# A first batch whose position bias and mask enter the scores as matrix products

## The chip, the cores and the metric

The kernel runs on one core of one Trainium2 chip. The metric is the device time of one execution in microseconds (us), less is better. Five engines work side by side, each through its own queue in order: TensorE (PE: matrix products and, as PEld, the loading of their stationary operand), VectorE (DVE), ScalarE (ACT), GpSimd (POOL) and SyncE (SP). POOL and SP also issue the DMA transfers here: POOL those that convert float32 to bfloat16 on the way, SP the plain ones.

## What is computed

Attention with a sliding window and a linear position bias, and behind it an MLP mixer that works first over tokens, then over channels:

```python
# q, k, v: (8 batches, 8 heads, 576 tokens, 64); window = 128, scale = 1/8
rel    = pos[:, None] - pos[None, :]
bias   = slopes[:, None, None] * (-abs(rel))             # slope of head h: 2 ** -(h + 1)
mask   = (rel >= 0) & (rel < window)
scores = where(mask, scale * q @ k.T + bias, -1e9)
attn   = softmax(scores)                                 # written out with exp, sum, divide
x      = (attn @ v), heads side by side                  # (8, 576, 512)
h      = relu(x.T @ w_tok1) @ w_tok2                     # over tokens, 576 -> 256 -> 576
u      = x + h.T
out    = u + relu(u @ w_ch1) @ w_ch2                     # over channels, 512 -> 1536 -> 512
```

## The kernel before

The 576 tokens of a batch are four blocks of 128 (kb, qb = 0..3) and a tail of 64. A block of queries sees two blocks of keys. A score tile is named Skbj: key block kb for the four heads of half j, 1024 columns in two PSUM banks (the last key block, kb = 3, also holds the tail's scores). ScalarE takes the exponential of a whole tile (into `pe`), and VectorE multiplies it by `masks` (into `pb`), which holds exp(-slope * distance) inside the window and 0 outside. `masks` is made once, by eight exponentials on ScalarE (names M0 to M3, two each) from `dist`, which GpSimd makes (J). `maskt` holds its columns for the tail (m0, m1, on VectorE).

Nothing is scheduled by a planner: the order is written by hand, as strings of names, one string for the start (PROLOGUE), one each for batch 0 with the rest of the start (FIRST), batch 1 (SECOND), batches 2 to 6 (PERIOD) and 7 (LAST). Each name is one small function that puts instructions into the queues of all engines that it uses; a quote mark behind a name means the next batch, two the one after it. So a name's place in the string is its place in every queue that it touches.

The names that matter in the start:

- q0, q1, l0, l1: loads of q and k of batch 0, heads 0 to 3, by SP as float32 (`qf0`, `kf0`); cq0, cq1 (VectorE) and ck0, ck1 (ScalarE) cast them. q23, l23, and with a quote mark q01', l01' and so on: loads by POOL. v0 to v4: loads of v. qt: the tails of q and k. LW: `W1`, `W1t` and `W2`. G0 to G2 and H0, H1: the channel weights `WC1` and `WC2`.
- A0 to A3, AT: transposes of q and k on TensorE, by head pair, with copies out of PSUM by VectorE and ScalarE (`pe_transpose`).
- s0, t0: tile S00 in two halves (`score_half`). S10 to S31: the other tiles. In batch 0, tiles in `S_M` lie in single banks `psM` and those in `SPLIT` get an exponential for each bank.
- p0 to p3: the products with v of batch 0 by head pair, with their divisions on VectorE; k0 to k3: the first token product and its relu; u0 to u3: the second one; x0 to x3: transposes of the result.
- W1 to W4: one to four products of zeros that keep TensorE running.
- O, e1, e2, ek, ex, FC: fills of constants, on VectorE (O, FC) and ScalarE (e1, e2, ek, ex).

PSUM has two score tiles `psS` of two banks, three single banks `psM` and one bank `psT`, each used in turn. In every batch, names C0 to C11 are the first channel product, D and E the second; `DVE_RELU` says which of C0 to C11 have their relu on VectorE, the others being on ScalarE. The tuples `x_DVE`, `k_DVE`, `AK_DVE`, `AQ_ACT`, `X_DVE`, `K_DVE` divide other copies and relus between these two engines.

Of the kernel before, what the change touches and what calls it, by code (L numbers as in the profile page):

```python
# [10 lines left out]
ACT = mybir.ActivationFunctionType  # L11
ALU = mybir.AluOpType
# [5 lines left out]
MASK_LATER = 1  # L18
U_DMA = (3, 4, 5, 6, 7)
U_ACT = (0, 1, 3)  # L20
X_DVE = (0, 1, 2)
K_DVE = (0,)
PROLOGUE = """
l0 I W2 q0 q1 J M3 l1 ck0 M0 W3 M1 W3 W3 l23 cq0 O qt m0 A0 q23 W3 v3 v0 ck1 v1 M2 FC W1 cq1 A1
s0 v2 S20 A2 t0 AT S10 A3 W2 S30 W2 S11 l01' v4 S01 q01' LW ex p0 G0 p1 W1 S21 m1 k0 S31 k1 q23'
l23' A1' e1 qt' W2 v4' ek p2 u0 A0' p3 G1 k2 S00' LC G2 u1 v1'
"""
FIRST = """
H1 v3' k3 u2 v2' x0 u3 A3' v0' W1 H0 A2' Lk'' UT x2 x1 AT' Lq'' S20' x3 Zq'' Zk'' Lk''' T0 S10'
S01' v3'' v0'' Lq''' C9 v0''' S21' C11 v4'' C3 e2 S31' C0 C5 S30' C7 C8 S11' C10 E0 C1 C2 v2''  # L30
C4 P2' v4''' C6 P3' D00 P0' P4' T1 E2 v1'' P1' D01 D02 K0' K1' D10 U1' v2''' D11 D12 U2' UT'
Zq''' X1' U0' U3' D20 D30 S11'' S20'' v1''' D21 D31 E1 Zk''' S00'' D22 S01'' D32
"""
SECOND = """
T1 X2 X0 X3 S30' S31' T0 C8 C9 C7 C11 C2 P0' C5 Lk''' C3 v0''' C4 v1''' C1 S21' S10' C10 Lq'''
# [11 lines left out]
"""  # L47
VROW = 96
NPB = 9
SPLIT = (1, 2)  # L50
S_M = (0, 2, 4, 5, 6)
S_P = ()
x_DVE = (1, 2, 3)
k_DVE = (2,)
AK_DVE = (2, 3, 7)
AQ_ACT = (1, 3, 4, 5, 7)
DVE_RELU = (2, 3, 4, 5, 7, 8, 10, 11)


@with_exitstack  # L60
def kernel(
# [11 lines left out]
    nc = tc.nc  # L73
    P = nc.NUM_PARTITIONS
    B, H, S, D = q.shape
# [3 lines left out]
    scale = 1.0 / math.sqrt(D)  # L79
    assert (B, H, S, D, DTOK, DCH) == (8, 8, 576, 64, 256, 1536)  # L80
    NC = S // P
    SM = NC * P
    ST = S - SM
    NHP = H // 2
    NHT = DCH // P
    NCB = DM // P
    slopes = [2.0 ** (-8.0 * (h + 1) / H) for h in range(H)]
# [5 lines left out]
    def T(name, shape, dt=bf16):  # L93
        return sb.tile(shape, dt, name=name, tag=name)
# [11 lines left out]
    def S2():  # L106

        t = psS[srot[0] % 2]
        srot[0] += 1
        return t  # L110

    def M():
        t = psM[mrot[0] % 3]
        mrot[0] += 1
        return t


    ident = T("ident", [P, P])
    qf0 = T("qf0", [P, 4, 4 * D], f32)
    kf0 = T("kf0", [P, 4, 4 * D], f32)  # L120
    zt = T("zt", [P, P])
    i2 = T("i2", [P, ST])
    dist = T("dist", [P, 2, P], f32)

    masks = T("masks", [P, 2, 2, 2, 2, P])

    maskt = T("maskt", [P, 2, 2, 2, 2, ST])
    W1 = T("W1", [P, NC, DTOK])
    W1t = T("W1t", [P, DTOK])
    W2 = T("W2", [P, 2, S])  # L130
# [11 lines left out]
    qT = [T(f"qT{i}", [P, NC + 1, NHP, P]) for i in range(2)]  # L142
    kT = [T(f"kT{i}", [P, NC + 1, NHP, P]) for i in range(2)]
    vp = [T(f"vp{i}", [P, NC + 1, H, VROW]) for i in range(3)]
    pe = [T(f"pe{i}", [P, 2, 512]) for i in range(3)]
# [18 lines left out]
    def later(n, fn):  # L164
        pend.append([n, fn])
# [96 lines left out]
    probs = {}  # L262
    half = {}

    def score_half(kb, a):

        def f():
            if a == 0:
                n = qrot[0]
                qrot[0] += 1  # L270
                half[kb] = (S2(), pe[n % len(pe)], pb[n % len(pb)])
                probs[0, kb, 0] = half[kb][2]
            s, e, p = half[kb]
            cs = slice(a * 256, (a + 1) * 256)
            for h in range(2):
                r = slice(h * D, (h + 1) * D)
                nc.tensor.matmul(s[:, h, cs], lhsT=kT[0][r, kb, a, :],
                                 rhs=qT[0][r, kb:kb + 2, a, :], start=True, stop=True)
            nc.scalar.activation(out=e[:, :, cs], in_=s[:, :, cs], func=ACT.Exp, scale=scale)

            def g():
                nc.vector.tensor_tensor(
                    out=p[:, :].rearrange("p (h x) -> p h x", h=2)[:, :, cs], in0=e[:, :, cs],
                    in1=masks[:, 0, :, a].rearrange("p h g x -> p h (g x)"), op=ALU.mult)
            later(MASK_LATER, g)
        return f
    tok1_banks = {}

    def score(b, kb, j):

        i = b % 2

        def f():
            n = qrot[0]
            qrot[0] += 1
            apart = j * 4 + kb in (S_M if b == 0 else S_P if b > 2 else ())
            t2 = None if apart else S2()
            s = [M(), M()] if apart else [t2[:, 0, :], t2[:, 1, :]]  # L300
            e = pe[n % len(pe)]
            p = pb[n % len(pb)]
            for a in range(2):
                hp = 2 * j + a
                halves = [slice(h * D, (h + 1) * D) for h in range(2)]
                if kb < NC - 1:
                    for h, r in enumerate(halves):
                        nc.tensor.matmul(s[h][:, a * 256:(a + 1) * 256], lhsT=kT[i][r, kb, hp, :],  # L308
                                         rhs=qT[i][r, kb:kb + 2, hp, :], start=True, stop=True)
                    continue  # L310
                for h, r in enumerate(halves):
                    nc.tensor.matmul(s[h][:, a * P:(a + 1) * P], lhsT=kT[i][r, kb, hp, :],  # L312
                                     rhs=qT[i][r, kb, hp, :], start=True, stop=True)
                for t in range(2):
                    for h, r in enumerate(halves):
                        c = 256 + t * P + a * ST
                        nc.tensor.matmul(s[h][:, c:c + ST], lhsT=kT[i][r, kb + t, hp, :],
                                         rhs=qT[i][r, NC, hp, 0:ST], start=True, stop=True)
            split = apart or b == 0 and j * 4 + kb in SPLIT
            parts = (slice(0, 1), slice(1, 2)) if split else (slice(0, 2),)  # L320
            for n, h in enumerate(parts):
                nc.scalar.activation(out=e[:, h, :], in_=s[n][:, None, :] if split else t2[:, :, :],  # L322
                                     func=ACT.Exp, scale=scale)
            probs[b, kb, j] = p

            def g():
                if kb < NC - 1:
                    for h in (parts if b == 0 else (slice(0, 2),)):
                        nc.vector.tensor_tensor(  # L329
                            out=p[:, :].rearrange("p (h x) -> p h x", h=2)[:, h], in0=e[:, h, :],  # L330
                            in1=masks[:, j, h].rearrange("p h g a x -> p h (g a x)"), op=ALU.mult)
                    return
                nc.vector.tensor_tensor(
                    out=p[:, 0:512].rearrange("p (h g x) -> p h g x", h=2, g=2),
                    in0=e[:, :, 0:256].rearrange("p h (g x) -> p h g x", g=2),
                    in1=masks[:, j, :, :, 0, :], op=ALU.mult)

                nc.vector.tensor_tensor(
                    out=p[:, 512:1024].rearrange("p (u h x) -> p h u x", u=4, h=2),
                    in0=e[:, :, 256:512].rearrange("p h (u x) -> p h u x", u=4),  # L340
                    in1=maskt[:, j].rearrange("p h t g x -> p h (t g) x"), op=ALU.mult)
            later(MASK_LATER, g)
        return f

    def prob(b, kb, h, nxt):

# [342 lines left out]
        return f  # L689

    def ones_v(i):
        nc.vector.memset(vp[i][:, :, :, D:D + 1], 1.0)
        nc.vector.memset(vp[i][ST:P, NC, :, 0:D + 1], 0.0)

    def load_w12():
        nc.gpsimd.dma_start(out=W1[:, :, :], in_=moe_w_tok1[0:SM, :].rearrange("(c p) d -> p c d", p=P))
# [18 lines left out]
    def make_dist():  # L715
# [4 lines left out]
        nc.gpsimd.affine_select(out=dist[:, :, :], in_=dist[:, :, :], compare_op=ALU.is_gt, fill=1.0e6,  # L720
                                base=P, pattern=[[-P, 2], [-1, P]], channel_multiplier=1)

    def load_wc1(g):
        nc.gpsimd.dma_start(
            out=WC1[:, :, g * 512:(g + 1) * 512],
            in_=moe_w_ch1[:, g * 512:(g + 1) * 512].rearrange("(j p) h -> p j h", p=P))

    def first_constants():
        nc.vector.memset(kT[0][:, NC, :, ST:P], 0.0)
        nc.vector.memset(hm[:, :], 0.0)  # L730
        nc.vector.memset(hm[0:D, 0:1], 1.0)
        nc.vector.memset(hm[D:P, 1:2], 1.0)

    def late_constants():
        nc.vector.tensor_copy(out=i2[0:ST, :], in_=ident[0:ST, 0:ST])
        nc.vector.tensor_copy(out=i2[ST:P, :], in_=ident[ST:P, ST:P])

    def fill_v(i):

        nc.scalar.activation(out=vp[i][:, :, :, D:D + 1].rearrange("p c h o -> p (c h o)"),  # L740
                             in_=zt[:, 0:(NC + 1) * H], func=ACT.Copy, bias=1.0)
        nc.scalar.copy(out=vp[i][ST:P, NC, :, 0:D + 1],
                       in_=zt[ST:P, None, 0:D + 1].broadcast_to([ST, H, D + 1]))

    def fill_k1():
        nc.scalar.copy(out=kT[1][:, NC, :, ST:P], in_=zt[:, None, 0:ST].broadcast_to([P, NHP, ST]))

    def fill_x1():
        nc.scalar.copy(out=xt[1][:, :].rearrange("p (a x) -> p a x", a=4),
                       in_=zt[:, None, :].broadcast_to([P, 4, P]))  # L750

    def load_f32(dst, src, hp):
        hs = slice(2 * hp, 2 * hp + 2)
# [13 lines left out]
    def names(b):  # L767
# [40 lines left out]
        if b == 0:  # L808
# [10 lines left out]
                d[f"ck{hp}"] = lambda hp=hp: cast_f32(nc.scalar.copy, ks, kf0, hp)  # L819
            d["LC"] = late_constants  # L820
            d["FC"] = first_constants
            d["e1"], d["e2"] = lambda: fill_v(1), lambda: fill_v(2)
            d["ek"], d["ex"] = fill_k1, fill_x1
            d["I"] = make_ident
            d["J"] = make_dist
            d["LW"] = load_w12
            d["O"] = lambda: ones_v(0)
            for kb in range(NC - 1):
                d[f"s{kb}"], d[f"t{kb}"] = score_half(kb, 0), score_half(kb, 1)
# [55 lines left out]
```

The softmax here doesn't subtract the row's maximum and nothing guards it: scores larger than these inputs give would overflow.

## Time and profile before

| | us |
|---|---|
| median of 4 runs | 290.82 |
| lowest, highest | 289.98, 291.38 |
| the profiled execution, its own time | 291.38 |
| span of its instructions in the profile | 289.7 |
| TensorE busy, share of the span | 97% |
| VectorE, ScalarE, GpSimd busy | 61%, 40%, 34% |
| granted TensorE clock, mean over the span | 0.994 |

A busy time is the sum of an engine's instructions with overlaps taken once. Matrix products are pipelined, so one has a duration of 379 ns for 512 columns in the profile while the next can start earlier than that; the distance between starts says what a product costs. "Chain" is the path of waits followed back from the last instruction.

### The profile page before, as it was taken

How to read it: one execution, taken by the hardware profiler on the slowest of the kernel's cores; microseconds unless marked ns; L12 is line 12 of the kernel's file. 1: busy time of each engine (PE TensorE's matmuls, PEld its weight loads, DVE VectorE, ACT ScalarE, POOL GpSimd, SP SyncE). 2: the span in 40 equal slices, each digit the busy share in tenths (PEclk: the TensorE clock that was granted, in tenths of full speed). 3: DMA queues.
4: the chain of work that ended last, by engine and by line, in shares of the span. 5: the costliest groups of instructions: out<-in, count | busy, mean ns of one | idle time of the engine just before them, and what ended most of it. 6: DMA issues, size and time to landing. Idle time of an engine off the chain costs nothing.

```text
span 289.7 us, 6456 instructions
## 1 busy us (share of the span) xinstructions
PE 281.0 (97%) x2707; PEld 155.6 (54%) x2707; DVE 177.5 (61%) x348; ACT 115.3 (40%) x176; POOL 99.5 (34%) x128
## 2 busy tenths in 40 slices
PE   8769999999999999999999999999999999999995
PEld 3348646546465556644655456644655456645543
DVE  3786687557677577556846467557846476426212
ACT  5878782137224532435341262435251263101300
POOL 8976543089309705920195004930000000000000
PEclk9998999999999999999999999999999999999999
DMA  7999999899999998998699976998703320061004
GB/s 176 167 199 193 198 184 138 150 158 142 132 204 152 160 223 105 137 173 150 145 117 166 141 175 90 132 156 204 120 2 93 99 65 2 36 111 72 2 36 145
DMA packets 148636, 38.00 MB, mean 131 GB/s; under 512 B 135808, under 2 KB 144128, under 8 KB 148608
## 3 DMA queue, kind: packets, MB, share of 16 engines
q0 software_dynamic: 103152, 17.41, 77.9%
q1 hardware_dynamic: 45456, 20.19, 32.0%
q8 instruction: 21, 0.34, 0.5%
q14 instruction: 7, 0.06, 0.1%
HBM read 35.85 MB, written 9.44 MB: 156 GB/s over the span
## 4 chain that ended last, share of the span: by engine, by line
PE 91%; DMA 4%; DVE 3%; issue 1%; POOL 1%; ACT 0%; SPq 0%
PE psM L501 29%; PE psM L549 28%; PE psM L434 4%; PE psM L459 4%; PE psS L308 4%; PE psT L516 4%; PE psM L571 4%; DMA W<-in_moe_w_tok_dram 3%; PE psS L373 2%; PE psS L369 2%; PE psS L401 1%; DMA qf<-in_q_dram 1%; PE psS L312 1%; PE psM L530 1%; PE psM L229 1%
## 5 line engine op out<-in xcount | busy, mean ns | idle before, releaser
L501 PE MATMUL psM<-utb,WC 128*128 128x512 bf16 x384 | 90.2, 379 | 0.0
L549 PE MATMUL psM<-WC,r 128*128 128x512 bf16 x372 | 86.5, 379 | 0.0
L322 ACT ACTIVATE pe<-psS 128x1024 bf16<-128x1024 f32 (+1 forms) x60 | 58.5, 1011 | 50.6 <-PE psS L308 44.3
L549 PEld LDWEIGHTS <-r 128*128 128x128 bf16 x372 | 34.5, 98 | 40.7 <-issue 3.2
L501 PEld LDWEIGHTS <-WC 128*128 128x128 bf16 x384 | 34.6, 98 | 37.6 <-issue 1.9
L504 DVE TENSOR_SCALAR r<-psM 128x512 bf16<-128x512 f32 x64 | 43.4, 687 | 15.0 <-PE psM L501 14.5
L185 POOL DMA_DIRECT2D kn<-in_k_dram x24 | 21.0, 892 | 81.6 <-DMA kT<-kn 76.6
L329 DVE TENSOR_TENSOR pb<-pe,masks 128x1024 bf16<-128x1024 bf16 (+1 forms) x52 | 32.8, 637 | 22.9 <-ACT pe L322 22.0
L554 DVE TENSOR_TENSOR ob<-psM,ub 128x512 f32<-128x512 f32 x31 | 21.4, 691 | 32.1 <-PE psM L549 32.0
L507 ACT ACTIVATE r<-psM 128x512 bf16<-128x512 f32 x32 | 19.1, 598 | 54.4 <-PE psM L501 53.8
L185 POOL DMA_DIRECT2D vp<-in_v_dram x32 | 29.2, 964 | 2.1 <-DMA WC<-in_moe_w_ch_dram 1.5
L185 POOL DMA_DIRECT2D qn<-in_q_dram x24 | 21.4, 945 | 3.4 <-DMA WC<-in_moe_w_ch_dram 2.9
L383 DVE TENSOR_TENSOR xb<-psS,rt 128x512 bf16<-128x512 f32 x28 | 19.4, 692 | 1.0
L461 DVE TENSOR_TENSOR ub<-psM,xb 128x512 bf16<-128x512 f32 x28 | 18.0, 685 | 2.1 <-PE psM L459 1.8
L373 PE MATMUL psS<-vp,pb 128*128 128x65 bf16 x224 | 15.7, 193 | 0.0
L373 PEld LDWEIGHTS <-pb 128*128 128x128 bf16 x224 | 13.6, 97 | 3.3
L459 PE MATMUL psM<-r,W 128*128 128x512 bf16 x56 | 15.4, 379 | 0.0
L516 PEld LDWEIGHTS <-WC 128*128 128x128 bf16 x384 | 13.2, 98 | 3.1
L519 ACT ACTIVATE r2t<-psT 128x384 bf16<-128x384 f32 x16 | 7.9, 491 | 17.4 <-PE psT L516 16.8
L308 PE MATMUL psS<-qT,kT 64*128 64x256 bf16 x172 | 14.5, 272 | 0.0
L516 PE MATMUL psT<-utt,WC 128*128 128x64 bf16 x384 | 13.8, 193 | 0.0
L434 PE MATMUL psM<-xb,W 128*128 128x256 bf16 x112 | 13.4, 273 | 0.0
(125 smaller groups left out, 294.5 us busy)
## 6 DMA issues: line engine op xcount, KB each, us to landing
out_dram<-ob SPq DMA_DIRECT2D x31, 256.0 KB, 2.2
vp<-in_v_dram POOLq DMA_DIRECT2D x32, 128.0 KB, 5.9
kn<-in_k_dram POOLq DMA_DIRECT2D x24, 128.0 KB, 4.4
qn<-in_q_dram POOLq DMA_DIRECT2D x24, 128.0 KB, 5.4
WC<-in_moe_w_ch_dram POOLq DMA_DIRECT2D x3, 512.0 KB, 9.2
WC<-in_moe_w_ch_dram POOLq DMA_DIRECT2D x2, 768.0 KB, 13.4
out_dram<-ob SPq DMA_DIRECT2D x10, 128.0 KB, 2.3
ks<-in_k_dram POOLq DMA_DIRECT2D x3, 256.0 KB, 5.8
```

The lines of the kernel that those rows point to most:

```text
L185: nc.gpsimd.dma_start(out=dst, in_=src[b, :, c * P:(c + 1) * P, :].rearrange("h s d -> s h d"))
L308: nc.tensor.matmul(s[h][:, a * 256:(a + 1) * 256], lhsT=kT[i][r, kb, hp, :], rhs=qT[i][r, kb:kb + 2, hp, :], start=True, stop=True)
L322: nc.scalar.activation(out=e[:, h, :], in_=s[n][:, None, :] if split else t2[:, :, :], func=ACT.Exp, scale=scale)
L329: nc.vector.tensor_tensor(out=p[:, :].rearrange("p (h x) -> p h x", h=2)[:, h], in0=e[:, h, :], in1=masks[:, j, h].rearrange("p h g a x -> ...
L373: nc.tensor.matmul(ov, lhsT=prob(b, qb, h, 0), rhs=vt[:, qb, h, 0:D + 1], start=first, stop=(hh == 3))
L434: nc.tensor.matmul(st["t"][h][:, dh * 256:(dh + 1) * 256], lhsT=W1[:, c, dh * P:(dh + 1) * P], rhs=by_half(xb[b % 2][:, c, :])[:, h], star ...
L459: nc.tensor.matmul(t[:, :], lhsT=W2[:, j, c * P:(c + 1) * P], rhs=r1[b % 2][:, j, :], start=(j == 0), stop=(j == 1))
L501: nc.tensor.matmul(t[:, :], lhsT=WC1[:, cb, ht * P:(ht + 1) * P], rhs=utb[b % 2][:, :, cb, :], start=(cb == 0), stop=(cb == NCB - 1))
L504: nc.vector.tensor_scalar(out=r2[b % 2][:, ht, :], in0=t[:, :], scalar1=0.0, scalar2=None, op0=ALU.max)
L516: nc.tensor.matmul(o, lhsT=WC1[:, cb, ht * P:(ht + 1) * P], rhs=utt[(b // 2) % 2][:, cb, b % 2, :], start=(cb == 0), stop=(cb == NCB - 1))
L549: nc.tensor.matmul(t[:, :], lhsT=r2[b % 2][:, ht, c * P:(c + 1) * P], rhs=WC2[:, ht, :], start=(ht == 0), stop=(ht == NHT - 1))
L554: nc.vector.tensor_tensor(out=o[:, :], in0=t[:, :], in1=ub[b % 2][:, c, :], op=ALU.add)
```

## The change

In batch 0 each score tile begins with products of another kind: a stationary matrix `sid[:, h]`, the identity times -slope(h)/scale, against `distb`, the distances in bfloat16 (1e6 outside the window), which starts the accumulation. The score products are then added to it, and the exponential of the sum, with scale, is written straight to `pb`. The mask product on VectorE is gone from batch 0; batches 1 to 7 keep it, so `masks` and `maskt` are still made, later in the order. Making `distb` and `sid` (B) is nine instructions on VectorE. The fills O, e1, e2, ek, ex and FC go to GpSimd. The strings PROLOGUE and FIRST have a new order, and the tuples that divide work between VectorE and ScalarE have new values, `DVE_RELU` and `X_DVE`, `K_DVE` for the later batches too.

```diff
-X_DVE = (0, 1, 2)
-K_DVE = (0,)
+X_DVE = (0, 1)
+K_DVE = (0, 1)
 PROLOGUE = """
-l0 I W2 q0 q1 J M3 l1 ck0 M0 W3 M1 W3 W3 l23 cq0 O qt m0 A0 q23 W3 v3 v0 ck1 v1 M2 FC W1 cq1 A1
-s0 v2 S20 A2 t0 AT S10 A3 W2 S30 W2 S11 l01' v4 S01 q01' LW ex p0 G0 p1 W1 S21 m1 k0 S31 k1 q23'
-l23' A1' e1 qt' W2 v4' ek p2 u0 A0' p3 G1 k2 S00' LC G2 u1 v1'
+q0 I J l0 W2 O l1 q1 B l23 W3 cq0 FC q23 W3 v1 ck0 v0 qt A0 v3 v2 W2 cq1 ck1 W3 A1 s0 A2 t0 S20
+AT S10 A3 S30 q01' W1 v4 l01' S01 LW G0 M2 e1 p0 S11 q23' ex ek W1 S21 M1 p1 M3 m1 M0 k0 m0 S31
+A1' W2 l23' W2 v1' k1 qt' p2 G1 A0' u1 G2 LC e2 p3 S00' u0
 """
 FIRST = """
-H1 v3' k3 u2 v2' x0 u3 A3' v0' W1 H0 A2' Lk'' UT x2 x1 AT' Lq'' S20' x3 Zq'' Zk'' Lk''' T0 S10'
-S01' v3'' v0'' Lq''' C9 v0''' S21' C11 v4'' C3 e2 S31' C0 C5 S30' C7 C8 S11' C10 E0 C1 C2 v2''
...
+v3' k2 v4' H0 k3 W1 x0 u2 u3 A2' v2' UT A3' v0' S20' x1 H1 Lk'' AT' Lq'' x3 Zq'' Zk'' T0 x2 S01'
+C9 Lk''' S30' C6 v0'' v3'' Lq''' C11 C5 v0''' S31' v4'' S10' C2 C3 E0 C8 S21' C10 S11' C0 P3' T1
...
-SPLIT = (1, 2)
-S_M = (0, 2, 4, 5, 6)
+SPLIT = (1, 3, 7)
+S_M = (2, 4, 6)
...
-x_DVE = (1, 2, 3)
-k_DVE = (2,)
-AK_DVE = (2, 3, 7)
-AQ_ACT = (1, 3, 4, 5, 7)
-DVE_RELU = (2, 3, 4, 5, 7, 8, 10, 11)
+x_DVE = (1, 2)
+k_DVE = (1, 3)
+AK_DVE = (0, 3, 5, 7)
+AQ_ACT = (1, 3, 7)
+DVE_RELU = (2, 4, 6, 9, 11)
...
+    distb = T("distb", [P, 2, P])
+    sid = T("sid", [P, H, P])
...
+    def bias(out, h, d, first=True):
+        nc.tensor.matmul(out, lhsT=sid[:, h, :], rhs=d, start=first, stop=False)
...
     def score_half(kb, a):
...
+            for h in range(2):
+                bias(s[:, h, cs], 2 * a + h, distb[:, :, :])
             for h in range(2):
...
-                                 rhs=qT[0][r, kb:kb + 2, a, :], start=True, stop=True)
-            nc.scalar.activation(out=e[:, :, cs], in_=s[:, :, cs], func=ACT.Exp, scale=scale)
-            def g():
-                nc.vector.tensor_tensor(
-                    out=p[:, :].rearrange("p (h x) -> p h x", h=2)[:, :, cs], in0=e[:, :, cs],
-                    in1=masks[:, 0, :, a].rearrange("p h g x -> p h (g x)"), op=ALU.mult)
-            later(MASK_LATER, g)
+                                 rhs=qT[0][r, kb:kb + 2, a, :], start=False, stop=True)
+            nc.scalar.activation(out=p[:, :].rearrange("p (h x) -> p h x", h=2)[:, :, cs],
+                                 in_=s[:, :, cs], func=ACT.Exp, scale=scale)
...
+        def first():
...
+            todo = []
+            for a in range(2):
+                if not last:
+                    todo.append((a, slice(a * 256, (a + 1) * 256), distb[:, :, :], kb,
+                                 qT[0][:, kb:kb + 2, 2 * j + a, :]))
+                    continue
+                todo.append((a, slice(a * P, (a + 1) * P), distb[:, 0, :], kb, qT[0][:, kb, 2 * j + a, :]))
+                for t in range(2):
+                    c = 256 + t * P + a * ST
+                    todo.append((a, slice(c, c + ST), distb[:, 1 - t, 0:ST], kb + t,
+                                 qT[0][:, NC, 2 * j + a, 0:ST]))
+            for n, (a, cs, d, _, _) in enumerate(todo):
+                for h in range(2):
+                    bias(s[h][:, cs], 2 * (2 * j + a) + h, d, n == 0)
+            for n, (a, cs, _, kk, qs_) in enumerate(todo):
+                for h, r in enumerate(halves):
+                    nc.tensor.matmul(s[h][:, cs], lhsT=kT[0][r, kk, 2 * j + a, :], rhs=qs_[r],
+                                     start=False, stop=(n == len(todo) - 1))
...
-        return f
+        return f if b else first
...
     def ones_v(i):
-        nc.vector.memset(vp[i][:, :, :, D:D + 1], 1.0)
-        nc.vector.memset(vp[i][ST:P, NC, :, 0:D + 1], 0.0)
+        nc.gpsimd.memset(vp[i][:, :, :, D:D + 1], 1.0)
+        nc.gpsimd.memset(vp[i][ST:P, NC, :, 0:D + 1], 0.0)
...
+    def make_bias():
+        nc.vector.tensor_copy(out=distb[:, :, :], in_=dist[:, :, :])
+        for h in range(H):
+            nc.vector.tensor_scalar(out=sid[:, h, :], in0=ident[:, :], scalar1=-float(slopes[h]) / scale,
+                                    scalar2=None, op0=ALU.mult)
...
     def first_constants():
-        nc.vector.memset(kT[0][:, NC, :, ST:P], 0.0)
+        nc.gpsimd.memset(kT[0][:, NC, :, ST:P], 0.0)
...
     def fill_k1():
-        nc.scalar.copy(out=kT[1][:, NC, :, ST:P], in_=zt[:, None, 0:ST].broadcast_to([P, NHP, ST]))
+        nc.gpsimd.memset(kT[1][:, NC, :, ST:P], 0.0)
     def fill_x1():
-        nc.scalar.copy(out=xt[1][:, :].rearrange("p (a x) -> p a x", a=4),
-                       in_=zt[:, None, :].broadcast_to([P, 4, P]))
+        nc.gpsimd.memset(xt[1][:, :], 0.0)
...
-            d["e1"], d["e2"] = lambda: fill_v(1), lambda: fill_v(2)
+            d["e1"], d["e2"] = lambda: ones_v(1), lambda: ones_v(2)
```

In batch 0's tiles of the last key block (kb = 3) the exponential is now four instructions of 256 columns for each tile, where it was one of 1024; the tiles S01, S21 and S20 are two of 512 as before, S10 too, and S11 is one of 1024 where it was two of 512.

## The prediction

> **What bounds the kernel now.** I read first the page's slices, to see which engine is full and when, then stretches of the span, then the chain and ScalarE's timeline of the first 27 us. Rows TensorE, ScalarE and granted clock of the page's slices (7.2 us each):
>
> ```profile
> PE   8769999999999999999999999999999999999995
> ACT  5878782137224532435341262435251263101300
> PEclk9998999999999999999999999999999999999999
> ```
>
> TensorE is short of full only in the first four slices, and there its clock dips. Stretches of the span (busy us and number of PE, PEld, DVE, ACT, POOL; then granted clock, DMA share, GB/s):
>
> ```profile
> 10.00:15.00 5.00, 4.32 (x66) 2.27 (x66) 4.11 (x10) 4.66 (x10) 5.00 (x8) 1.00 2.10 167
> 15.00:20.00 5.00, 2.65 (x47) 1.75 (x47) 4.74 (x16) 3.60 (x8) 2.83 (x5) 1.00 1.39 199
> 20.00:25.00 5.00, 5.00 (x74) 3.87 (x72) 2.28 (x8) 4.11 (x8) 3.39 (x5) 0.66 1.43 195
> ...
> 36.00:250.00 214.00, 214.00 (x2026) 117.16 (x2026) 140.43 (x262) 82.94 (x113) 72.75 (x87) 1.00 1.21 133
> ```
>
> From 36 to 250 us TensorE has no hole, and the list of waits has none of its own there. So what VectorE or ScalarE is spared later is worth nothing, and what the start loses or wins goes to the end one for one. The hole is at 15 to 20 us, and the stretch behind it runs at 0.66 of the clock. The chain of the first 36 us, in order of time (start, length, what):
>
> ```profile
> 1.32 3.15 DMA qf<-in_q_dram
> ...
> 8.60 0.64 PE psM L229 x16
> ...
> 11.96 7.40 DMA W<-in_moe_w_tok_dram
> 19.40 0.40 PE psM L641 x4
> ...
> 25.16 0.57 PE psM L229 x16
> 25.73 0.17 PE psS L602 x2
> ...
> 26.32 0.07 PE psS L609
> ...
> 33.16 0.33 PE psS L308 x4
> ...
> 33.81 0.70 PE psT L516 x24
> ```
>
> k0 (L641) waits until 19.4 for W1, which stands behind all of batch 0 in POOL's queue. 26.39, the end of p3 (L609), is my mark: behind it TensorE has the same list to do in both kernels, except that u0 stands for u1. ScalarE's timeline:
>
> ```profile
> 2.66 0.72 ACT L703 ACTIVATE masks<-dist 128x256 bf16<-128x256 f32 x2 [0.58 <-POOL dist L720]
> 4.32 1.33 ACT L703 ACTIVATE masks<-dist 128x256 bf16<-128x256 f32 x4
> 14.04 1.02 ACT L322 ACTIVATE pe<-psS 128x1024 bf16<-128x1024 f32 x1
> 14.96 2.06 ACT L322 ACTIVATE pe<-psM 128x512 bf16<-128x512 f32 x4
> 20.94 1.02 ACT L322 ACTIVATE pe<-psS 128x1024 bf16<-128x1024 f32 x1 [0.17 <-PE psS L317]
> ```
>
> The mask exponentials lie before 9 us, where nothing else wants ScalarE; the one for S31 is over at 21.96. Unit prices: 0.33 us for 256 columns, 0.51 for 512, about 1.0 for 1024, 0.52 for a copy of 512.
>
> **The change, part by part.** *Added on TensorE.* 48 bias products: 24 of 256 columns (S00 to S21), 8 of 128 and 16 of 64 (S30, S31). A batch of 64-column products runs at 0.70/24 = 0.03 us each (L516), a 512-column product in the full stretch at 0.216, so 0.108 for 256 and 0.054 for 128. Sum 2.6 + 0.4 + 0.5 = 3.5 us. A tile then costs 0.33 (L308 x4) + 0.43, and about 0.1 for the change between full and half rows: 0.85. Fillers fall from 23 to 20 products; they stand in holes, worth nothing by themselves.
>
> *Taken from VectorE.* Batch 0's mask products. One or two of them (0.4 to 0.85 us) stood between the last exponential of a tile and the product with v that needs it; p0 and p2 now follow ScalarE directly. The walk below has that in it.
>
> *Fills.* O moves to POOL ahead of l23: on VectorE 0.09 and 0.49 us. POOL's own fills are 0.20 us for 128 columns and 0.10 for one, so about 0.5 for 520; I take 0.6 us for the pair, at least 0.2, at most 1.3 (double). FC's four follow l23 (about 0.5). e1, ex, ek and e2, about 2 us, fall where POOL waits for transfers to finish (0.4 to 1.7 us at a time between 16 and 36 us): 0, as the transfers lag their issue by 6 to 9 us. Were that lag gone, up to 2 us.
>
> *B.* No row shows 128 to 128 columns on VectorE; 64 columns took 0.18, 256 took 0.37 to 0.56. I take 0.15 to 0.3, with `distb` 1.6 to 2.8 us from 2.65 on: cq0 starts at 4.3 to 5.5 where it was 4.49. The Trainium skill (SBUF — State Buffer, Who interferes with whom) says that VectorE's copies and tensor_scalar in two-port modes and GpSimd shut each other out for a whole instruction. The trace has cq0 beside POOL's issues at 0.65 us and cq1 at 0.83: at most 0.2 more. By the rule B might wait for O, 0.6 us, and cq0 start at 4.9. Both give 0: A1 needs q1, which is now SP's fourth load, and the fourth landed at 2.33 + 5.0 = 7.3.
>
> *Now the walk.* cq1 7.3 to 7.95, A1 at 8.05 (was 8.60). A2 needs q23. It landed at 10.86 behind l23 and the two tails; without these 128 KB it comes 0.7 us sooner (167 to 195 KB per us), with POOL's later start 0.2 to 0.6 later: 10.4. v1, v0 and qt (384 KB) follow, so qt lands at 12.6. TensorE: A2 10.4 to 10.97 (0.57), t0 to 11.5, S20 to 12.35, AT 12.6 to 12.95, S10 to 13.8, A3 to 14.4, S30 to 15.25, filler, S01 to 16.3.
>
> ScalarE, from S20 on without a hole: S20 12.5 to 13.5; AT's copy 13.8; S10 14.0 to 15.0; A3's copy 15.55; S30, now four of 256 (1.36), 16.9; S01 17.95; M2 (two masks) 18.6; S11 19.6; S21 20.6; **six masks (M1, M3, M0), 2.0, to 22.6**; k0's relu 23.0; S31, again four, 24.35. TensorE beside it: p0 16.95 to 17.5, S11 to 18.35, S21 to 19.4, p1 to 19.95, k0 to 20.6 (W1, behind the same bytes and POOL's later start, lands near 19.7 and is no longer the last), S31 to 21.45, A1' to 22.0, four fillers to 22.9; k1 needs k0's bank, which the relu frees at 23.0: to 23.65. p2 waits for S31's exponentials until 24.4, then p2 (0.55), A0' (0.57), u1 (0.67), p3 (0.55): p3 ends at 26.75. Against 26.39: +0.36.
>
> Behind p3, VectorE is late next. Before it does p3's divisions (1.35 us in the trace for p2's) it has p2's (25.05 to 26.4), A0's copy (0.69) and two small copies (0.6), so they end at 29.05; TensorE, with S00', u0 and k2 (1.7 us), wants k3 at 28.5: +0.45, between 0 and 0.6. C9 needs G2, which came over 2 us ahead of it; 64 KB more in front is 0.3 us: 0. Three more relus of each batch go from VectorE (0.69) to ScalarE (0.60), which is 39% busy from 36 to 250 us: 0, up to 0.3 us a batch if they queue behind exponentials. X2's copy and k-relus: same answer.
>
> *Clock.* The trace halves the clock after a hole of 1.7 us at 17.7. The Trainium skill (TensorE: Matmul & The Clock Gate, Part 1) puts half clock after an idle window of about 3.4 us. By the rule no stretch of either kernel would be slow; by the row the old hole costs 3.4 us at half clock, up to 1.7 us, and the new holes (0.75 at most, before p2) cost none. I take the row; but what it wins, from k0 to p2, is lost again in the wait for ScalarE.
>
> Sum on the profiled execution (291.38, span 289.7): +0.36 + 0.45 = +0.8, 292.2. It lies 0.56 above the median of the runs, so 291.6.
>
> **The rivals.** *Faster: TensorE fills its hole and ScalarE isn't last.* For it: the hole and the slow stretch are real, and the bias products fit them. If q23 lands at 9.8 and S31's exponentials end a microsecond or more sooner, TensorE's own order sets p2 at 22.8 and p3 ends near 25.1 to 25.3: own time 290.2, reported 289.6. Against it: ScalarE's 11.5 us from S20 to S31 have no hole. It decides when S31's last exponential ends before about 23.4.
>
> *Much slower: POOL's fills.* If O takes over a microsecond, or the lock of the rule holds each for long, l23 and all behind it land 1 us later, A2 slips to 11.2 or more, and a hole long enough to halve the clock from p2 to p3 (2.3 us of work) adds to it: +2.2, own 293.6, reported 293.0. For it: POOL is full from 10 to 15 us. Against: the DMA queue is backed up by then.
>
> *ScalarE late in every batch* by the moved relus: eight times 0.2 to 0.3, +2, reported 293. Against: with three more relus a batch ScalarE has some 96 us of work in those 214.
>
> *The change doesn't do what it says*: excluded, the built program has the 48 products and no mask product in batch 0; TensorE has 45 products more in all.
>
> **How the numbers follow.** ScalarE's queue sets p2: 0.50, reported 290.6 to 292.6 (q23 0.4 either way, POOL's bounds, k3). TensorE's own order: 0.22. POOL's fills or clock: 0.23. Relus: 0.05. A measurement of this kernel can tell about 0.3% (0.9 us). Of the first case 0.2 lies inside that and 0.3 above it; the second is faster, the last two slower: 0.22, 0.20, 0.58. The range leaves out half of the faster case and the upper part of the slow ones: 289.2 to 293.8.
>
> **What would show it.** Right: in the profile after, ScalarE without a hole from 12.5 to 24.4 with six mask exponentials ahead of S31; the wait of p2 (now L646) put down to ScalarE; k0 no more waiting for W1 for 1.7 us; the clock full from 20 to 25; p3's end near 26.75. Wrong: p3's end before 25.9 (then ScalarE had room), A2 after 11.2 (POOL), or a wait of TensorE after 36 us (relus).

## The result, and the profile after

The changed kernel takes 291.59 us (median of 36 runs, 290.65 to 293.32), the one before, timed beside it, 290.57 (57 runs, 289.5 to 291.97). The profiled execution of the kernel after took 291.76 us, with a span of 290.0 and a mean clock of 0.994. The ratio is 1.0035, 95% interval 1.0025 to 1.0044: the change makes it slower by 1.0 us. The forecast was 291.6, by +0.8.

The rows of TensorE, ScalarE and granted clock in the page's slices of the kernel after (7.25 us each):

```profile
PE   8699999999999999999999999999999999999995
ACT  4597875048414561435341291436341291103300
PEclk9899999999999999999999999999999999999999
```

TensorE is short of full only in the first two slices, where it was in the first three, and the dip of the clock has moved from the fourth slice to the second. Stretches of the span, in the columns used ahead (busy us and number of PE, PEld, DVE, ACT, POOL; then granted clock, DMA share, GB/s):

```profile
10.00:15.00 5.00, 4.49 (x46) 2.40 (x48) 0.98 (x2) 2.65 (x6) 5.00 (x8) 0.69 2.05 153
15.00:20.00 5.00, 5.00 (x82) 3.24 (x78) 1.97 (x5) 4.85 (x12) 4.87 (x9) 0.97 1.43 188
20.00:25.00 5.00, 5.00 (x110) 4.22 (x110) 3.57 (x12) 4.41 (x14) 4.74 (x8) 1.00 1.34 204
36.00:250.00 214.00, 213.65 (x2022) 116.82 (x2017) 131.55 (x246) 88.27 (x127) 73.03 (x88) 1.00 1.20 133
```

TensorE had 2.65 us of work from 15 to 20 us; now it has 5.00. The stretch at a reduced clock, 20 to 25 us before, is now 10 to 15 us (0.69). VectorE is relieved (131.55 against 140.43 us from 36 to 250 us) and nothing comes of it. The list of TensorE's waits (total us, times, longest):

```profile
PE psM L231 <- DMA qs<-in_q_dram: 2.4, 1, 2.4
PE psT L731 <- DVE zt L726: 1.1, 1, 1.1
PE psM L256 <- DMA qkt<-in_k_dram: 0.4, 1, 0.4
PE psM L545 <- DMA utb<-ub: 0.3, 1, 0.3
PE psS L353 <- DVE qT L236: 0.2, 1, 0.2
```

The wait for W1 (1.7 us ahead of k0) has gone and a wait for q23 (A2, L231), 0.6 us before, has grown to 2.4. The 0.3 us at L545 is one transfer at 133 us; it is absent in several of the kernels below and explains nothing. TensorE's timeline around the first wait:

```profile
10.13 0.41 PE L231 MATMUL psM<-ident,qs 128*64 128x128 bf16 x8 [2.37 <-DMA qs<-in_q_dram]
...
12.81 0.59 PE L256 MATMUL psM<-ident,qkt 128*128 128x128 bf16 x4 [0.38 <-DMA qkt<-in_k_dram]
13.19 1.06 PE L269 MATMUL psS<-distb,sid 128*128 128x256 bf16 x4
...
16.66 0.60 PE L269 MATMUL psM<-distb,sid 128*128 128x256 bf16 x4
17.19 0.39 PE L323 MATMUL psM<-qT,kT 64*128 64x256 bf16 x4
...
20.56 0.39 PE L685 MATMUL psM<-xb,W 128*128 128x128 bf16 x4
...
22.57 1.04 PE L731 MATMUL psT<-zt 128*128 128x512 bf16 x4
...
24.47 0.23 PE L651 MATMUL psS<-vp,pb 128*128 128x130 bf16 x1
...
26.42 0.22 PE L653 MATMUL psS<-vp,pb 128*128 128x130 bf16 x1
26.87 0.40 PE L353 MATMUL psS<-qT,kT 64*128 64x256 bf16 x4 [0.23 <-DVE qT L236]
```

A2 starts at 10.13, k0 (L685) at 20.56, with no wait. The bias products of S10 at 13.19 take 1.06 us in the slow stretch, those of S01 at 16.66 take 0.60. S01 then goes to its score products 0.53 us after its start, and these cost 0.33. And ScalarE's timeline:

```profile
21.08 1.96 ACT L748 ACTIVATE masks<-dist 128x256 bf16<-128x256 f32 x6
22.92 0.40 ACT L694 ACTIVATE r<-psM 128x256 bf16<-128x256 f32 x1
23.18 0.41 ACT L332 ACTIVATE pb<-psS 128x256 bf16<-128x256 f32 x1
...
23.97 0.44 ACT L335 ACTIVATE pb<-psS 128x256 bf16<-128x256 f32 x1
```

Six masks, then k0's relu, then S31's four exponentials, the last over at 24.41. That is the queue that the prediction wrote out. The two products of p2 that read S31 start at 24.47 and 24.54. The last product of p3 ends at 26.64 (26.39 before). Of the chain of waits, in order of time, these pieces (start, length, what):

```profile
8.39 4.29 DMA qkt<-in_k_dram
...
21.22 1.83 ACT masks L748 x6
...
25.93 0.29 DVE xt L671
26.22 0.61 DVE qT L236
26.87 0.40 PE psS L353 x4
```

The tails' load, the six masks and VectorE's copy ahead of S00' (L353) are in the chain, where before it was W1. From the masks the chain goes on through VectorE (`maskt`, then copies and p2's divisions), not through S31's exponentials.

### The profile page after: what moved, and what is told of

The parts are those of the page before. It is cut to its first block, busy times and chain, and to the rows that moved or that the text cites. A ratio compares the mean times of both kernels' runs of the same rounds, so it can differ in the third digit from the quotient of the medians.

```text
span 290.0 us, 6553 instructions
## 1 busy us (share of the span) xinstructions
PE 282.2 (97%) x2752; PEld 157.1 (54%) x2752; DVE 161.9 (56%) x318; ACT 119.6 (41%) x192; POOL 103.3 (36%) x140
## 4 chain that ended last, share of the span: by engine, by line
PE 87%; DMA 4%; POOL 2%; DVE 2%; ACT 2%; issue 1%; SPq 0%; POOLq 0%
PE psM L545 29%; PE psM L593 25%; PE psM L478 4%; PE psT L560 4%; PE psM L503 4%; PE psS L353 4%; PE psM L615 4%; DMA utb<-ub 3%; PE psS L417 2%; PE psS L413 2%; DMA qkt<-in_k_dram 1%; PE psS L445 1%; ACT pb L329 1%; PE psM L574 1%; PE psS L357 1%; ACT masks L748 1%
## 5 line engine op out<-in xcount | busy, mean ns | idle before, releaser
L545 PE MATMUL psM<-utb,WC 128*128 128x512 bf16 x384 | 90.0, 379 | 0.3 <-DMA utb<-ub 0.3
L367 ACT ACTIVATE pe<-psS 128x1024 bf16<-128x1024 f32 x56 | 54.9, 1031 | 41.8 <-PE psS L353 41.5
L545 PEld LDWEIGHTS <-WC 128*128 128x128 bf16 x384 | 34.6, 97 | 38.1 <-issue 2.3
L551 ACT ACTIVATE r<-psM 128x512 bf16<-128x512 f32 x56 | 32.3, 620 | 51.9 <-PE psM L545 51.9
L373 DVE TENSOR_TENSOR pb<-pe,masks 128x1024 bf16<-128x1024 bf16 x42 | 28.6, 690 | 20.9 <-ACT pe L367 20.9
L548 DVE TENSOR_SCALAR r<-psM 128x512 bf16<-128x512 f32 x40 | 27.1, 688 | 10.4 <-PE psM L545 10.2
L494 DVE TENSOR_SCALAR r<-psM 128x512 bf16<-128x512 f32 x14 | 9.0, 686 | 17.6 <-PE psM L487 17.6
L353 PE MATMUL psS<-qT,kT 64*128 64x256 bf16 x168 | 14.3, 272 | 0.2 <-DVE qT L236 0.2
```

The costliest lines, as they stand in the source:

```text
L373: nc.vector.tensor_tensor(out=p[:, :].rearrange("p (h x) -> p h x", h=2), in0=e[:, :, :], in1=masks[:, j].rearrange("p h g a x -> p h (g a ...
L545: nc.tensor.matmul(t[:, :], lhsT=WC1[:, cb, ht * P:(ht + 1) * P], rhs=utb[b % 2][:, :, cb, :], start=(cb == 0), stop=(cb == NCB - 1))
L548: nc.vector.tensor_scalar(out=r2[b % 2][:, ht, :], in0=t[:, :], scalar1=0.0, scalar2=None, op0=ALU.max)
L551: nc.scalar.activation(out=r2[b % 2][:, ht, :], in_=t[:, :], func=ACT.Relu)
```

## The experiments

Theories after the result. **A**: ScalarE's queue, with the masks late in it, sets p2, as predicted. **B**: TensorE's own queue from A2 on, longer by the bias products, sets it. **C**: the new shares of relus cost a little in each batch. **D**: the fills on GpSimd delay the loads. The granted clock became a fifth while the runs went on. All ratios are to the kernel before on the same chip, timed in the same rounds.

### The kernel before once more

> The kernel before, unchanged, for a second profile and the spread. Any theory: ratio 1.000, within 0.15%. If the stretch at half clock (20.4 to 23.8 us in the first profile) depends on where the start falls against a free-running window, it lies elsewhere or is missing here, and k0 still starts near 19.4 us, when W1 lands.

Ratio 1.0008 (0.9992 to 1.0025), 290.91 us. Its profile is not the first one again. The slow stretch now lies behind the wait for q23:

```profile
10.00:15.00 5.00, 4.10 (x52) 2.23 (x54) 3.43 (x9) 3.07 (x7) 4.49 (x7) 0.66 2.09 166
15.00:20.00 5.00, 3.53 (x63) 2.04 (x60) 3.91 (x13) 4.38 (x8) 2.77 (x5) 1.00 1.39 199
20.00:25.00 5.00, 4.96 (x105) 3.96 (x103) 4.12 (x15) 4.50 (x10) 3.40 (x5) 1.00 1.43 195
```

k0's row in its TensorE timeline:

```profile
19.80 0.38 PE L641 MATMUL psM<-xb,W 128*128 128x128 bf16 x4 [0.79 <-DVE rtt L626]
```

k0 starts at 19.80, waits 0.79 us for VectorE and not for W1, and p3 ends at 25.38, a microsecond sooner than in the first profile. So a slow stretch at 11 to 15 us costs the kernel before less than one at 20 to 24 us, behind k0: part of it goes into the wait ahead of k0. It is not free either. In e11 below, whose profile has no slow stretch at the start, p3 ends at 24.65, another 0.7 us sooner. The mark of 26.39 that the prediction measured against belonged to one execution with the slow stretch in the bad place.

### Masks early (theory A)

```diff
-q0 I J l0 W2 O l1 q1 B l23 ...  A1 s0 A2 ...  G0 M2 e1 ... S21 M1 p1 M3 m1 M0 k0
+q0 I J l0 W2 O l1 q1 B M0 M1 l23 ...  A1 s0 M2 M3 A2 ...  G0 e1 ... S21 p1 m1 k0
```

> The kernel after, with the eight mask exponentials moved to where ScalarE is idle (four before ck0, four behind s0). Theory A (ScalarE's queue with six masks ahead of S31 sets p2): p3 ends 0.4 to 0.6 us earlier, time 0.4 to 0.6 us below after. Theory B (from A2 on TensorE's own queue is full: bias products and fillers behind the late loads): S31's exponentials end 1.5 to 2 us earlier in the profile, but p2 starts at the same 24.0, time within 0.2 us of after. Theory C (shares of ScalarE in later batches) and D (POOL's fills): same as after.

Ratio 1.0037 (1.0021 to 1.0052), no gain. ScalarE was indeed relieved; its timeline shows S31's exponentials a microsecond earlier and ScalarE waiting for TensorE:

```profile
21.43 0.38 ACT L694 ACTIVATE r<-psM 128x256 bf16<-128x256 f32 x1
22.23 0.38 ACT L332 ACTIVATE pb<-psS 128x256 bf16<-128x256 f32 x1 [0.41 <-PE psS L323]
...
23.03 0.40 ACT L335 ACTIVATE pb<-psS 128x256 bf16<-128x256 f32 x1
```

p3 ends at 26.70 (after: 26.64), no sooner. A alone falls.

### No fillers (theory B, its cheapest part)

The first five W's behind AT, seven products of zeros in all, are taken out.

```diff
-... q01' W1 v4 ... ek W1 S21 ... A1' W2 l23' W2 v1' ... k3 W1 x0
+... q01' v4 ... ek S21 ... A1' l23' v1' ... k3 x0
```

> The kernel after without the seven filler products that stand from S30 on (1.5 us of TensorE in order). Theory A: p2 waits for S31's exponentials near 24.4 as before, time within 0.3 us of after. Theory B: TensorE's queue comes out shorter, up to the point where ScalarE's relu of k0 or S31 binds: p3 ends 0.5 to 1.0 us earlier, time 0.5 to 1.0 below after. C and D: same as after, or slower if the clock falls.

Ratio 1.0039 (1.0024 to 1.0054), no gain either. Its list of TensorE's waits shows what took the fillers' place: k1 waits for k0's relu, which stands behind the six masks.

```profile
PE psM L685 <- ACT r L694: 1.0, 1, 1.0
...
PE psS L353 <- DVE qT L236: 0.5, 1, 0.5
```

So both chains end together in the kernel after: k1 starts behind the fillers at 23.45, and k0's relu, which stands behind ScalarE's masks, is over at 23.32.

### Both together

> The kernel after with the masks early and without the seven fillers, both at once. If the fillers only fill a wait for ScalarE (relu of k0 at 23, S31's exponentials to 24.4), each alone gives nothing and both together give 0.6 to 1.0 us: about 290.7. If ScalarE and fillers are no cause at all (bias products behind the late loads, then divisions on VectorE set p3 and k3): within 0.3 us of after, 291.3 to 291.9.

The two edits above in one kernel: ratio 1.0017 (0.9998 to 1.0036), 291.08 us.

```profile
25.64 0.22 PE L653 MATMUL psS<-vp,pb 128*128 128x130 bf16 x1
26.32 0.40 PE L353 MATMUL psS<-qT,kT 64*128 64x256 bf16 x4 [0.45 <-DVE qT L236]
```

p3 ends at 25.86. That is 15.0 us after the start of A2, where the kernel after takes 16.5, e2 16.2 and e3 16.4, each with one slow stretch in between: at this mark only both edits together gain. S00' then waits 0.45 us for VectorE. How much reaches the time isn't clear: by the ratio half of the loss comes back, but at full clock (the table below) e5 is only 0.2 us below the kernel after, in five executions.

### The old shares (theory C)

```diff
-X_DVE = (0, 1)
-K_DVE = (0, 1)
-DVE_RELU = (2, 4, 6, 9, 11)
+X_DVE = (0, 1, 2)
+K_DVE = (0,)
+DVE_RELU = (2, 3, 4, 5, 7, 8, 10, 11)
```

> The kernel after with DVE_RELU, X_DVE and K_DVE of before. Theory C (more relus on ScalarE cost in every batch): about 1 us below after. Theories A, B, D: within 0.2 us of after, with no wait of TensorE behind 36 us in either, but for a transfer's jitter.

Ratio 1.0054 (1.0037 to 1.0070), slower if anything; its executions at full clock have a median of 291.25 us, those of the kernel after 291.29. The new shares cost nothing. C falls.

### Batch 0's products in the wait for q23

```diff
-... A1 s0 A2 t0 S20 AT S10 A3
+... A1 s0 t0 S20 S10 A2 AT A3
```

> The kernel after with t0, S20 and S10 ahead of A2: their products, bias among them, need nothing of the load that A2 waits for (7.5 to 10.1 us). Theory B (the bias products cost because they stand behind A2's wait): 2.2 us of TensorE go into the wait, the clock does not fall at 11 us, p0 starts near 15.5 and k0 then waits for W1 near 19.9 instead of starting at 20.6: 0.7 to 1.2 us below after. Theory A (late masks on ScalarE): ScalarE's queue starts sooner too, and the same 0.5 to 1.0. If only the loads and VectorE set the start: 0 to 0.3.

Ratio 1.0007 (0.9992 to 1.0022), 291.06 us: by the ratio most of the loss comes back. In the profile A2 goes to 11.22 and the wait behind it moves to the tails (AT, 1.7 us), and p3 ends at 26.99, since that execution had its slow stretch from 15.2 to 18.6 us. But in 21 of its 22 executions the mean clock was 0.998 or more, where 22 of 37 of the kernel after have about 0.994 or less. That made the clock a theory.

### Without the bias products

The 48 products are left out, and with them batch 0's bias and mask in the result.

> The kernel after without its 48 bias products (the score products start the sums; position bias and mask of batch 0 are left out of the result). Theory B: TensorE's queue from A2 to S31 is 3 us shorter, down to the wait for W1 (19.9) and what stands behind it: 0.7 to 1.5 us below after. Theory A: S31's exponentials still end near 23.5 behind the masks: at most 0.4 below after.

Ratio 1.0012 (0.9996 to 1.0028), 0.7 us below the kernel after by the two ratios, for 48 products less. 19 of its 22 executions had a mean clock below 0.9915. An emptier TensorE was a slower TensorE, so this run cannot price the products; e12 below does.

### The fills of O and FC back on VectorE (theory D)

```diff
-        nc.gpsimd.memset(vp[i][:, :, :, D:D + 1], 1.0)
+        eng = nc.vector if i == 0 else nc.gpsimd
+        eng.memset(vp[i][:, :, :, D:D + 1], 1.0)
...
-        nc.gpsimd.memset(kT[0][:, NC, :, ST:P], 0.0)
+        nc.vector.memset(kT[0][:, NC, :, ST:P], 0.0)
```

> The kernel after with the fills O and FC on VectorE again (O behind cq0). Theory D (GpSimd's fills in front of the loads delay A2): q23 lands 0.4 to 0.6 us earlier and all behind it, 0.4 to 0.6 below after. Other theories: A2 0.3 to 0.6 earlier in the profile, but time within 0.3 of after.

O also moves behind cq0 in the order. Ratio 1.0003 (0.9983 to 1.0022): by the ratio faster, but not by D's mechanism. TensorE's timeline:

```profile
8.66 0.41 PE L231 MATMUL psM<-ident,qs 128*64 128x128 bf16 x8 [1.68 <-DVE qs L804]
...
10.40 0.41 PE L231 MATMUL psM<-ident,qs 128*64 128x128 bf16 x8 [0.57 <-DMA qs<-in_q_dram]
```

q23 came no sooner (A2 at 10.40, against 10.13), so no delay by GpSimd's fills is seen. Where A2 waits for q23 it starts anywhere from 10.13 to 11.06 in the profiles of the kernel after and its variants, so one profile can't exclude the few tenths that D forecast. What differs is A1, made late by the fills on VectorE, which splits one wait of 2.4 us into 1.7 and 0.6, and this profile has no slow stretch. Its wide interval does not separate that from other small gains, and at full clock it is still 0.8 us slower than the kernel before (the table below).

### The wait for q23 filled

```diff
-... A1 s0 A2 t0 S20
+... A1 s0 W4 W4 A2 t0 S20
```

> After, with eight more products of zeros (0.216 us each, some 1.7 us) put into TensorE's queue ahead of A2, that is into its wait of 2.4 us for q23; nothing else moves. Theory clock (the half-clock window that starts behind this wait costs 0.4 to 0.8 us in after, as it lies in a stretch where TensorE has no slack): no window at 11 to 15 us in most runs, 0.3 to 0.8 us below after, ratio to before 1.001 to 1.003. Theory products (the 3.5 us of bias products behind A2 are the whole loss): as after, ratio 1.0035. Rival (the fillers make A2 late): A2 after 10.4 us and above after.

Ratio 1.0016 (1.0002 to 1.0029), 291.27 us: by the ratio half of the loss comes back from products that compute nothing. All 22 executions ran at full clock; against the executions of the kernel after that did so too (291.29) nothing is gained. In this profile q23 landed late, and its own time of 291.78 lies above the kernel's median. The row of A2:

```profile
11.06 0.41 PE L231 MATMUL psM<-ident,qs 128*64 128x128 bf16 x8 [0.99 <-DMA qs<-in_q_dram]
```

### Everything named so far, in one order

Masks M0 and M1 early, S20 and S10 ahead of A2, qt right behind q23, p0 to p3 and S31 ahead of k0, eight fillers in other places for seven of them, another order of batch 0's first C's, and some of batch 0's and 1's copies and relus moved from VectorE to ScalarE.

```diff
-... B l23 ... A1 s0 A2 t0 S20 AT S10 A3 S30 ... k0 m0 S31 A1' ... p3 S00' u0
+... B M0 M1 l23 ... A1 s0 t0 S20 S10 v2 v4 A2 A3 AT S01 S30 ... S31 M2 M3 W4 p2 p3 W2 A1' l23' k0 ...
```

> After with all causes that the runs have named so far taken together: two masks made early, S20 and S10 ahead of A2 in TensorE's queue (2.2 us of batch 0's products into the wait for q23), qt's transfer right behind q23, the tiles S11, S21, S31 and the products p0 to p3 ahead of batch 1's transposes and of k0, one to four fewer fillers around k0, and of batch 0's first channel products those that need the late half of WC1 first. Theory (only the order of TensorE's queue from 8 to 26 us holds after back): A2 at 11.2, k0 and p3 both done by 25, first C before 33.8 with S10' done: 1.5 to 3 us below before, ratio 0.990 to 0.995. Rival, loads: W1, q23' and G1 come no sooner, TensorE waits for them instead, within 0.5 us of before. Rival, ScalarE: p2 waits for S31's exponentials as before, no gain.

Ratio 1.0026 (1.0013 to 1.0038): the 1.5 to 3 us expected of it are not there. Every execution ran at full clock, and the waits are short but spread out. Its list:

```profile
PE psM L231 <- DVE qs L803: 1.1, 2, 0.6
PE psT L731 <- DVE zt L726: 1.1, 1, 1.1
PE psS L269 <- ACT pb L286: 0.7, 1, 0.7
PE psM L231 <- DVE qT L236: 0.6, 2, 0.4
PE psS L269 <- DVE xt L671: 0.5, 1, 0.5
```

W1 and q23 no longer appear; in their place t0 waits for the exponential of s0 (L286), a transpose for VectorE's copy (L236) and S31 for VectorE's last piece of p1's division (L671). With the loads out of the way, round trips between the engines are what TensorE waits for. It doesn't beat the kernel before, and the kernel after not clear of noise.

### The kernel before, with its waits filled

```diff
-s0 v2 S20 A2 t0 ... W1 S21 m1 k0 S31
+s0 v2 S20 W4 A2 t0 ... W1 S21 m1 W4 W2 k0 S31
```

> Before, with ten more products of zeros in two of TensorE's waits: four ahead of A2, six ahead of k0 (0.86 and 1.3 us); nothing else moves. Theory (the slow-clock window of 3.4 us behind a wait costs before 0 to 0.9 us by where it falls, and the waits ahead of k0 are slack): full clock in most runs, 0.4 to 0.8 us below before, ratio 0.9972 to 0.9988, which is below after too. Rival (the window is hidden in the slack anyway): ratio 1.000. Rival (the fillers delay A2 and k0): above 1.000.

290.53 us, ratio 0.9988 (0.9960 to 1.0016). 11 of 12 executions ran at full clock, as expected, but the interval is too wide to call it faster. The row of granted clock on its page:

```profile
PEclk9999999999999999999999999999999999999999
```

There is no dip left where the kernel before had one.

### Without the bias products, waits filled

e7's kernel (batch 0's bias and mask again left out of the result), with eight products of zeros ahead of A2, four ahead of AT and four ahead of k0.

> After without the 48 bias products (batch 0's bias and mask are left out of the result), with 16 products of zeros in the waits that this opens: eight ahead of A2, four ahead of AT, four ahead of k0 (1.7, 0.86 and 0.86 us). It costs the bias products at a full clock, which the kernel without them and without fillers, mostly at a slower clock, could not. Theory (3.4 us of bias products, of which 2.5 us lie in waits and some 0.9 us on the path): full clock in most runs, 0.9 to 1.5 us below after, at or up to 0.5 us below before, ratio to before 0.998 to 1.000. Rival (the loss is in the rest of the change: fills on GpSimd, later masks, the order, VectorE's shares): at after, ratio 1.002 to 1.004.

290.56 us, ratio 0.9988 (0.9965 to 1.0012), level with e11 on the same chip. 11 of 12 executions at full clock.

### The clock, over all runs

Executions of one kernel differ in how many stretches of 3.41 us at half clock the start has, which their mean granted clock tells (1.00 none, about 0.994 one, about 0.988 two; in some a piece of half clock at the very end lowers it by 0.001 to 0.003). Median us by that, with the number of executions:

| kernel | none | one | two |
|---|---|---|---|
| before (beside e1 to e4) | 290.07 (25) | 290.86 (47) | 292.04 (3) |
| before (beside e5 to e8) | 290.07 (17) | 291.03 (30) | 292.24 (11) |
| before (beside e9, e10) | 289.92 (10) | 290.91 (33) | |
| before (beside e11, e12) | 290.42 (6) | 291.28 (14) | 291.98 (3) |
| before again, e1 | 289.76 (4) | 290.91 (14) | 292.26 (4) |
| after | 291.29 (15) | 291.76 (21) | 293.11 (1) |
| masks early, e2 | 291.47 (7) | 291.69 (13) | 293.35 (2) |
| no fillers, e3 | 291.32 (6) | 291.95 (16) | |
| old shares, e4 | 291.25 (5) | 292.36 (14) | 293.45 (3) |
| both, e5 | 291.11 (5) | 291.03 (8) | 293.48 (1) |
| products in the wait, e6 | 291.03 (21) | 291.73 (1) | |
| no bias, e7 | | 290.84 (3) | 291.32 (19) |
| fills back, e8 | 290.85 (10) | 291.75 (4) | |
| wait filled, e9 | 291.27 (22) | | |
| reordered, e10 | 291.38 (22) | | |
| before filled, e11 | 290.49 (11) | 290.89 (1) | |
| no bias, filled, e12 | 290.48 (11) | 292.60 (1) | |

The rows come from several chips; at full clock the kernel before has 290.07, 290.07, 289.92 and 290.42 on four of them, so differences under some 0.4 us between rows mean little. A slow stretch costs 0.5 to 1.2 us in most rows (0.2 in e2, nothing in e5), not the 1.7 that half of 3.41 us would be, so part of it seems to fall into waits.

At full clock the kernel after is still 1.2 us slower than the one before. And at full clock every variant that keeps the bias products is still 0.8 (e8) to 1.5 us (e10) above the kernel before on its own chip: e5 and e6 at 1.0, e9 at 1.35. None of these is clear of the kernel after. So what the ratios of e6, e8 and e9 gained on the kernel after is for the larger part the clock: their own (21 of 22 executions without a slow stretch in e6, 22 of 22 in e9), and, beside e5 to e8, that of the kernel before, which had two slow stretches in 11 of 58 executions there, against 3 of 75 beside e1 to e4. The clock therefore isn't the reason for the loss; fillers take the slow stretches out, and the loss stays.

What comes before a slow stretch can be read from the profiles too. Nine of them have one in the first 27 us. The 3.41 us just ahead of it hold 0.8 to 1.7 us of TensorE's work (kernel before 1.65, after 1.74, e1 1.66, e5 0.81). Counted on in steps of 3.41 us from a piece at half clock, others with as little work were followed by full clock (e7 1.71, e8 1.73). In the first 30 us none with 2.0 us or more was followed by a slow one, but for e4's second stretch, which follows on its first. By these figures it is not the length of the wait alone that counts, but how much of it falls into one such piece; where the boundary lies is not shown.

The price of the bias products follows from e9 and e12, both at full clock: 291.27 less 290.48 is 0.8 us; by the ratios to before, 1.0016 less 0.9988, it is 0.28% (0.8 us too, with some 0.8 us of uncertainty). Against the full-clock executions of before on their own chips, e9 is at +1.35 (289.92) and e12 at +0.06 (290.42). In TensorE's queue the 48 products take 4.5 us (e9's profile, from the start of each group to that of the score products behind it; 3.5 us by their columns alone). So of 4.5 us 0.8 to 1.3 us reach the end, the second with about a microsecond either way, and the rest goes into waits. The whole remainder of the change (fills, order, shares, no mask products) comes to about nothing within these bounds. e12 has eight more fillers than e9 besides, in waits that the missing products open.

## Why the prediction was right, and where it wasn't

- **TensorE's start goes to the end one for one**: held. From 36 us on there is no wait but one transfer of 0.3 us, and from k3's start to the end of the span it is 261.8 and 261.6 us in the two profiles of before, 261.6 after. (Of the slices before, three and not four are short of full.)
- **Bias products 3.5 us, a tile 0.85**: held for the tile: S01 takes 0.53 + 0.33 = 0.86. The 3.5 us count columns alone; with the change between full and half rows, which the price of the tile has in it, the products come to 4.5 us.
- **B, cq0, A1**: cq0 at 4.04 (predicted 4.3 to 5.5), A1 at 6.58 (8.05), 1.5 us sooner, as q1 had landed. A2 at 10.13 (10.4), AT at 12.81 (12.6 to 12.95), k0 at 20.56 (20.6). W1 is no longer last: held.
- **The longest new hole 0.75 us, and no slow clock**: failed. TensorE was done early and empty for 2.37 us ahead of A2, and a stretch at half clock follows from 11.87 to 15.28. The walk itself had about 1.3 us between the end of s0 and A2, so the 0.75 did not fit it. By the table this costs some 0.5 us in 22 of 37 executions.
- **p2 waits for S31's exponentials, 24.4; p3 ends at 26.75**: right in its times (exponentials over at 24.41, p3 at 26.64), half right in its cause. With ScalarE a microsecond sooner (e2) p3 didn't move; with TensorE's fillers gone (e3) k1 waited for ScalarE. The two chains were level, which a forecast from one "last" wait can't show; only e5 moved both. Of the signs named ahead two are missing: ScalarE is idle for 1.02 us until 14.83, and p2 has no wait put down to ScalarE. The fillers were put at nothing, as standing in holes; seven of them stand in this full queue.
- **k3 waits 0.45 for VectorE**: not there, k3 starts at 28.44 unhindered. S00' waits 0.2 instead, for the copy of A0' that stands behind p2's divisions on VectorE. p3's divisions are over at 28.47, not 29.05: the sum took whole durations of copies, which in the queue start closer together.
- **+0.36 at p3's mark**: this term was sized against one execution of before. It measured +0.25 against that one (26.39), and +1.26 against the other profile of before (25.38). At k3's start, where both kernels have done the same list again, the kernel after is 0.57 us behind the first profile and 1.23 behind the second; 0.81 was forecast. So the sum of 0.8 met the measured 1.0 with one term that didn't come (k3, 0.45) and one that it didn't have (the slow stretch of the kernel after, 0.5 in most executions). Its total was right, its division wasn't, and that they met is in part luck.
- **The old slow stretch costs up to 1.7 us**: too much. One slow stretch costs the kernel before 0.8 to 1.2 us by the table.
- **Row or rule for the clock**: the row was nearer in one thing. The Trainium skill (TensorE: Matmul & The Clock Gate, Part 1) puts half clock behind an idle window of about 3.4 us; here half clock came after waits of 1.5 us (e1) and 2.4 us, with up to 1.7 us of work in the 3.41 us ahead of it. The same part says that the window runs free and the same kernel varies between runs. That agrees with the table, each slow stretch being 3.41 us long and placed differently from run to run. Reading the rule as far as that sentence would have told that one profile doesn't show where the slow stretch lies.
- **GpSimd's fills 0.6 us for O, 0 in the time**: 0.30 and 0.56 us (`vp`, 128x40 and 64x520), 0.86 together and inside the stated bounds; q23 came no sooner without them (e8). **Relus of the later batches 0**: held (e4). The rival of fast TensorE needed S31's exponentials before 23.4; e2 gave 23.43, and it didn't get faster, so the point from which it was to decide was wrong: by TensorE's own queue p2's last product starts at 24.60 there too.

What stays open: why e10, with the long waits gone, isn't faster than e9. Its short waits are named above, none was taken out by itself. How much of e5's gain at p3 reaches the end. And whether e11's 0.6 us is a gain.

## What to carry to other kernels

When work moves to the engine that bounds the kernel, count how much of it fits into that engine's waits and how much stands behind the last of them: here all but 0.8 to 1.3 of 4.5 us fitted, and the rest was the loss, while the engines that were relieved held TensorE up nowhere from 36 us on. Before naming the one engine that a wait ends on, ask which chain is next and how close it is: two level chains show no gain until both are shortened, as e2, e3 and e5 do at p3's mark. Compare variants at the same clock, too: four of the ratios here looked like gains, and at full clock none was clear of the kernel after. And take a second profile of the kernel before you measure a forecast against a mark in its first, above all where the clock isn't full.

## What the runs showed of the hardware

Products of zeros have a use beyond keeping time. Eight of them in a wait of 2.4 us changed the share of executions with a full clock from 15 of 37 to 22 of 22 (e9, on another chip), ten in two waits of the kernel before from 6 of 23 to 11 of 12 (e11, on the same chip). Taking work away from TensorE did the reverse: without the bias products and with nothing in their place (e7), 19 of 22 executions had two slow stretches, where 11 of 58 of the kernel before on the same chip and 1 of 37 of the kernel after do. So e7, with 48 products less, is only 0.7 us below the kernel after.
